# Chunked attention with a gated convolution on one core: the first head-pair group taken by halves, the start of a written-out order rearranged, and 27 GpSimd steps given a wait on VectorE

## The chip, the cores and the metric

The kernel runs on one core of a Trainium2 chip. The metric is the device time of one execution in microseconds (us); several runs of each kernel are made, and the median is compared. Four compute engines of the core appear below by the names of the profile: PE is TensorE (PEld its weight loads), DVE is VectorE, ACT is ScalarE, POOL is GpSimd. SP is the queue that issues every DMA of this kernel.

## What is computed

Attention inside chunks of 64 tokens, then a gate from a causal convolution of five taps and two projections:

```python
scores = scale * np.matmul(q_c, k_c.transpose(0, 1, 2, 4, 3))
scores = scores - np.max(scores, axis=-1, keepdims=True)
attn = np.exp(scores)
attn = attn / (np.sum(attn, axis=-1, keepdims=True) + 1e-09)
out = np.matmul(attn, v_c)
...
for k in range(K):
    gate_pre += conv_w[k][None, None, :] * xp[:, k:k + S, :]
gate = 1.0 / (1.0 + np.exp(-gate_pre))
val = x @ w_val
return (gate * val @ w_out).astype(np.float32)
```

q, k and v have 8 batches, 8 heads, 576 tokens and 64 features in float32; x is the attention's output with the heads side by side (512 features). The weights are 512 x 512 and arrive as 64-bit floats that the kernel turns into 32-bit ones itself.

## The kernel before

The 4608 tokens are taken in nine groups `g` of 512 tokens (0 to 8), and the 512 features in two pairs of 128-row blocks, `p` = 0 and 1. One (g, p) is called a pair here. The program is a list of short pieces, `ORDER`, 1034 of them, run in the order in which they are written. A piece is a name and numbers, and each engine executes its own instructions in that order. Nothing is reordered afterwards, so the table alone sets who stands behind whom on each engine. `SLOTS` gives every tile its buffer, also by hand: `z` tiles are 128 x 1024 in SBUF, `b` tiles are PSUM banks. A piece that reuses a buffer waits for the last reader of what was there. All instructions go through one helper, `run` (line 139 of the profile), so every row of the profile carries that line, and the tiles tell the rows apart.

The pieces of one pair, in the order of its data:

- `lq`, `lk`, `lv`: DMAs of q, k and v, 512 KB each (256 KB for a half). SP lets eight DMAs be under way; a ninth waits until the first has landed.
- `S g p b`: scores of one half b (16 products of 64 x 64, which the trace records as 32 matmuls).
- `mx`: the row maximum (DVE). Then one of two ways to the exponentials: `sb` subtracts the maximum (DVE) and `ex` takes one exponential over all (ACT); or `ng` negates the maximum (DVE) and `ea` takes eight or sixteen exponentials of 64 columns with the maximum as bias and the row sums as a by-product (ACT).
- `sm` (sum and reciprocal on DVE) or `rc` / `ra` and `rr` after `ea`: one over the row sums.
- `nm`: exponentials times that (POOL). `T`: transposes of the result (PE). `ec`: copy out of PSUM (ACT).
- `A`: attention times v (PE). `xr`, `xd`: the result as a rounded high part (ACT) and the rest (DVE); `xc`: a plain copy for the convolution (ACT, or DVE as `xcD`).
- `V g m c`: three (or, with a fourth number, one) products of 128 x 128 by 512 for the value projection; `P` the same for the output projection; `vc`, `gs`, `gr`, `gd`, `oc`, `st`: the gate, its two parts, the output copies and stores.
- `k0`, `k`, `kk`: the five taps (ACT for the first, DVE for the others), `sg` the sigmoid.

The weights go through `lw` (load), `w1` to `w4` (bits of the 64-bit float to a 32-bit one; `w2` on ACT, the others on DVE), `w5` and `w8` (the remainder), `w6` (rounded high part), `wa` and `wb` or `Q` and `wc` (the low part, the second way by PE). A letter `D` behind a name means that the piece runs on DVE. `n c` behind it is the matrix (`v` or `o`) and its quarter.

In the kernel before, pair (0, 1) goes by halves from the scores to the values, with `ng`/`ea` for both halves, and pair (0, 0) goes as a whole: one `mx`, one `sb`, one `ex`, one `sm`, one `nm`, one `T`, one `A`. `W 9 22` and `W 3` are products of a constant tile that no result needs.

The tables before and now both end in the same 602 pieces; what differs lies ahead of these.

Of the kernel before, what the change touches and what calls it, by code (L numbers as in the profile page):

```python
# [18 lines left out]
ORDER = """zw,lw v 1,zr 1,zr 0,lc,zi,zs 0,zs 1,lw v 3,lw v 2,w1 v 1,w5 c 0,w1 c 0,w2 v 1,w3 v 1,w5 v 1,w4 v 1,w2 c 0,w3 c 0,w5 v 3,  # L19
w7 v 1,w1 v 3,w6 v 1,w8D v 1,w2 v 3,w4 c 0,w3 v 3,W 9 22,Q v 1,lk 0 1 0,lq 0 1 0,w1 v 2,w4 v 3,w2 v 2,w3 v 2,w5 v 2,w6D v 3,  # L20
S 0 1 0,lk 0 0 0,lk 0 1 1,lq 0 1 1,lq 0 0 0,lk 0 0 1,lq 0 0 1,w4 v 2,wc v 1,mx 0 1 0,w6 v 2,w7 c 0,ng 0 1 0,w7 v 2,ea 0 1 0,ra 0 1 0,
W 3,S 0 1 1,w8D v 2,S 0 0 0,mx 0 1 1,w8D c 0,w9,ng 0 1 1,w7 v 3,S 0 0 1,lw v 0,lk 1 0,lq 1 0,lv 0 1,lw o 3,ea 0 1 1,ra 0 1 1,
rr 0 1 0,Q v 2,w8 v 3,mx 0 0,nm 0 1 0,sb 0 0,Q v 3,w5 v 0,w1 v 0,ex 0 0,T 0 1 0,w3 v 0,rr 0 1 1,S 1 0 0,wc v 2,sm 0 0,
nm 0 1 1,S 1 0 1,ec 0 1 0,w2 v 0,A 0 1 0,lk 1 1,lq 1 1,lv 0 0,lv 1 0,wc v 3,mx 1 0,T 0 1 1,nm 0 0,xr 0 1 0,ec 0 1 1,
V 0 2 2 0,sb 1 0,V 0 3 2 1,w5 o 3,A 0 1 1,xc 0 1 0,xr 0 1 1,w4 v 0,T 0 0,xc 0 1 1,xd 0 1 0,V 0 2 3 0,w6D v 0,V 0 3 3 0,
ec 0 0,V 0 2 3 1,w1 o 3,S 1 1 0,w7 v 0,ex 1 0,xd 0 1 1,A 0 0,w8 v 0,k0 0 2,sm 1 0,S 1 1 1,wa v 0,xc 0 0,V 0 0 2 0,V 0 2 2 1,
V 0 0 3 1,V 0 0 2 1,xr 0 0,mx 1 1,V 0 1 2 0,nm 1 0,V 0 0 3 2,V 0 3 3 1,k0 0 0,V 0 3 2 2,V 0 2 3 2,xd 0 0,V 0 3 1 0,
V 0 1 2 1,V 0 0 0 0,V 0 3 3 2,V 0 3 0 0,lw o 0,lw o 2,lw o 1,w5 o 0,k0 0 3,ng 1 1,k 0 0 1,T 1 0,k0 0 1,wbD v 0,V 0 0 0 2,
w2 o 3,V 0 3 2 0,k 0 0 2,V 0 2 1 1,ec 1 0,V 0 2 0 0,V 0 0 1 0,k 0 3 1,V 0 1 0 0,V 0 2 0 1,ea 1 1,V 0 2 0 2,w3 o 3,V 0 2 1 2,
k 0 1 1,V 0 3 1 1,V 0 0 2 2,V 0 1 1 1,w4 o 3,V 0 3 0 1,V 0 2 2 2,V 0 3 1 2,w1 o 1,A 1 0,k 0 0 3,w7 o 3,w1 o 0,V 0 1 3 2,  # L30
# [7 lines left out]
xd 2 0,vc 1 1,S 3 1 0,w4 o 0,S 3 1 1,ec 2 1,waD o 3,V 2 0 0,gs 0 0,xc 2 0,A 2 1,w6 o 0,w7 o 0,V 2 2 0,gs 0 1,xr 2 1,V 2 0 1,
lk 8 1,lq 5 1,w8 o 0,xd 2 1,V 2 1 0,V 2 2 1,ex 3 0,xcD 2 1,wa o 0,V 2 3 2,k0 1 0,V 2 3 0,sm 3 0,wb o 0,gr 0 0,S 4 0 0,
S 4 0 1,k0 1 2,mx 3 1,nm 3 0,V 2 2 2,gr 0 1,V 2 0 2,mx 4 0,k0 1 1,V 2 0 3,w6 o 2,hc 0 0,ng 3 1,hc 1 0,sb 4 0,hc 0 1,V 2 2 3,  # L40
wb o 3,ea 3 1,V 2 1 3,gdD 0 0,V 2 1 2,T 3 0,k 1 1 1,V 2 1 1,lv 4 0,lk 5 1,lk 7 0,lq 4 1,lk 4 1,lv 3 0,lk 5 0,lv 8 0,waD o 2,
V 2 3 1,wbD o 2,V 2 3 3,gdD 0 1,ec 3 0,S 4 1 0,S 4 1 1,rc 3 1,vc 2 0,k 1 1 2,A 3 0,ex 4 0,nm 3 1,mx 4 1,P 0 2 0,w5 o 1,
# [624 lines left out]
```

## Time and profile before

| | before |
|---|---|
| runs | 279.8, 280.34, 280.35 us; median 280.34 |
| span of the profiled execution (its first to its last instruction) | 279.6 us |
| its own time | not measured apart; the three runs lie 0.2 to 0.75 us above the span |
| PE busy | 268.9 us, 96% |
| DVE, ACT, POOL busy | 239.5, 198.7, 59.4 us |
| chain that ended last | PE 89%, DMA 8% |
| DMA | 42.46 MB, about 406 GB/s up to 49 us |
| granted PE clock | 1.00 over the span |

The page gives, for one profiled execution, the busy time of each engine, the span in slices, the DMA queues, and the chain of waits followed back from the last instruction. A matmul's end in the trace is modelled, so its duration (some 400 ns for 512 columns) is longer than the distance from one start to the next (some 230 ns): what PE can do is read from starts. "Issue" is idle time for which the profile shows no releaser.

### The profile page before, as it was taken

How to read it: one execution, taken by the hardware profiler on the slowest of the kernel's cores; microseconds unless marked ns; L12 is line 12 of the kernel's file. 1: busy time of each engine (PE TensorE's matmuls, PEld its weight loads, DVE VectorE, ACT ScalarE, POOL GpSimd, SP SyncE). 2: the span in 40 equal slices, each digit the busy share in tenths (PEclk: the TensorE clock that was granted, in tenths of full speed). 3: DMA queues.
4: the chain of work that ended last, by engine and by line, in shares of the span. 5: the costliest groups of instructions: out<-in, count | busy, mean ns of one | idle time of the engine just before them, and what ended most of it. 6: DMA issues, size and time to landing. Idle time of an engine off the chain costs nothing.

```text
span 279.6 us, 7851 instructions
## 1 busy us (share of the span) xinstructions
PE 268.9 (96%) x3370; PEld 216.6 (77%) x3370; DVE 239.5 (86%) x303; ACT 198.7 (71%) x368; POOL 59.4 (21%) x58
## 2 busy tenths in 40 slices
PE   6598999999998999999999999999999999999995
PEld 3366778887886888888888888888888888888884
DVE  3979999999999988989898998999999998996020
ACT  5899999999997988895958588837644544614402
POOL 1056242049294003061335001100000000300000
PEclk9999999999999999999999999999999999999999
DMA  6999999763831649540082000000000000050656
GB/s 224 395 409 406 406 407 409 290 225 108 281 149 37 192 150 338 189 131 30 2 292 88 2 5 2 0 0 2 0 0 0 4 0 0 16 212 0 241 209 225
DMA packets 14754, 42.46 MB, mean 152 GB/s; under 512 B 1536, under 2 KB 1792, under 8 KB 14720
## 3 DMA queue, kind: packets, MB, share of 16 engines
q1 hardware_dynamic: 14720, 41.97, 40.7%
q8 instruction: 26, 0.43, 0.6%
q14 instruction: 8, 0.07, 0.1%
HBM read 32.53 MB, written 9.44 MB: 150 GB/s over the span
## 4 chain that ended last, share of the span: by engine, by line
PE 89%; DMA 8%; issue 1%; SPq 0%; ACT 0%
PE b L139 89%; DMA z<-in_v 4%; DMA z<-in_moe_w_val 2%; DMA z<-in_q 2%; SPq L139 0%; ACT z L139 0%
## 5 line engine op out<-in xcount | busy, mean ns | idle before, releaser
L139 PE MATMUL b<-z,v_hi 128*128 128x512 f32 x288 | 97.3, 403 | 1.3 <-issue 1.1
L139 PE MATMUL b<-o_hi,z 128*128 128x512 f32 (+1 forms) x296 | 94.5, 391 | 0.0
L139 DVE SCALAR_TENSOR_TENSOR ys<-ys,cw 128x511 f32<-128x511 f32 (+7 forms) x104 | 84.5, 863 | 0.1
L139 ACT COPY z<-b 128x1024 f32<-128x1024 f32 (+2 forms) x53 | 50.3, 970 | 38.3 <-PE b L139 35.5
L139 PEld LDWEIGHTS b<-z,v_hi 128*128 128x128 f32 x288 | 53.8, 188 | 14.5 <-issue 1.7
L139 PEld LDWEIGHTS b<-o_hi,z 128*128 128x128 f32 x296 | 55.1, 188 | 12.6
L139 PE MATMUL b<-o_lo,z 128*128 128x512 f32 (+1 forms) x148 | 57.4, 388 | 0.0
L139 PE MATMUL b<-z,v_lo 128*128 128x512 f32 x144 | 55.9, 394 | 0.0
L139 POOL TENSOR_TENSOR z<-e_row,rs 128x1024 f32<-128x1024 f32 (+1 forms) x15 | 27.0, 1804 | 47.2 <-DVE rs L139 17.0
L139 PEld LDWEIGHTS b<-o_lo,z 128*128 128x128 f32 x148 | 27.8, 188 | 5.9
L139 PEld LDWEIGHTS b<-z,v_lo 128*128 128x128 f32 x144 | 27.1, 188 | 5.4
L139 POOL TENSOR_TENSOR z<-ys,z 128x1024 fp32r<-128x1024 f32 x4 | 10.0, 2527 | 96.9 <-ACT z L139 96.9
L139 ACT ACTIVATE ys<-ys 128x1024 f32<-128x1024 f32 x16 | 16.8, 1059 | 11.0 <-DVE ys L139 10.8
L139 ACT ACTIVATE e_row<-b,mx 128x64 f32<-128x64 f32 x80 | 23.7, 345 | 0.4 <-DVE mx L139 0.4
L139 DVE TENSOR_TENSOR z<-b,z 128x1024 fp32r<-128x1024 f32 (+1 forms) x19 | 22.0, 1161 | 2.3 <-ACT z L139 1.3
L139 ACT CAST z<-ys 128x1024 fp32r<-128x1024 f32 x16 | 16.5, 1048 | 9.0 <-DVE ys L139 9.0
L139 DVE TENSOR_REDUCE mx<-b 128x16 f32<-128x1024 f32 (+1 forms) x19 | 21.6, 1144 | 1.3 <-PE b L139 1.1
L139 PEld LDWEIGHTS b<-z,z 64*64 64x64 f32 x960 | 15.7, 135 | 7.8 <-DMA z<-in_k 2.6
L139 PE MATMUL b<-z,z 64*64 64x64 f32 x960 | 17.6, 221 | 3.7 <-DMA z<-in_q 3.0
L139 ACT CAST z<-b 128x1024 fp32r<-128x1024 f32 (+1 forms) x19 | 18.7, 991 | 2.1 <-PE b L139 2.1
L139 ACT ACTIVATE ys<-ys,cw 128x512 f32<-128x512 f32 (+1 forms) x25 | 19.2, 811 | 0.0
L139 ACT ACTIVATION_READ_ACCUMULATOR e_row<-b,mx 128x1 f32 x80 | 19.0, 238 | 0.0
(74 smaller groups left out, 308.3 us busy)
## 6 DMA issues: line engine op xcount, KB each, us to landing
out<-z SPq DMA_DIRECT2D x16, 512.0 KB, 3.7
z<-in_q SPq DMA_DIRECT2D x10, 512.0 KB, 7.2
z<-in_v SPq DMA_DIRECT2D x9, 512.0 KB, 5.0
ys<-in_v SPq DMA_DIRECT2D x9, 512.0 KB, 10.1
ys<-in_k SPq DMA_DIRECT2D x9, 512.0 KB, 7.3
z<-in_k SPq DMA_DIRECT2D x7, 512.0 KB, 9.4
ys<-in_q SPq DMA_DIRECT2D x6, 512.0 KB, 10.2
z<-in_moe_w_val SPq DMA_DIRECT2D x4, 512.0 KB, 5.4
```

Source lines behind the costliest of these rows:

```text
L139: return tc.keep_in_program_order(fn(*args, **kwargs))
```

## The change

- Pair (0, 0) goes by halves too: `mx`, `sb`, `ex`, `sm`, `nm`, `T`, `ec`, `A`, `xr`, `xd`, `xc` and its `lv` are two pieces each. Its `xc` runs once on DVE and once on ACT.
- Half 0 of pair (0, 1), and the pair (2, 0), go to the exponentials in a third way: `mh` splits the maximum into two rounded parts (two small DVE steps), `M` subtracts them from the scores in PSUM by four matmuls against minus the identity, and `exM` takes one exponential straight from PSUM. `M 0 1 0` has 256 columns each, `M 2 0` 512. This replaces `ng`, `ea`, `ra`, `rr` there, and `sb`, `ex` in (2, 0). Half 1 of (0, 1) keeps `ng` and `ea`, with `rc` for `ra` and `rr`.
- Weights: `w1G` is `w1` on POOL (value quarter 0, output quarters 0, 1, 2); `w58` is `w5` and `w8` in one DVE step (value quarter 1, output quarters 1, 2, 3); `w6`, `wa`, `wb` of some quarters change engine. One `nm` (3, 1) and one `k0` go to DVE, two `xc` (2, 1) and (3, 0) to ACT.
- The pieces ahead of the common tail stand in another order, SP's loads among them: q ahead of k, both ahead of value quarter 0; the halves of v (0, 0) ahead of k and q (1, 1); the loads of groups 2 and up mixed differently; v (1, 0) four loads later than before, counted in bytes.
- `SLOTS` is new throughout, and the tile `ys` holds the buffers from 28 up and no longer from 20 up.
- `BEHIND`: 27 pieces on POOL (`gd`, `nm`, `w1G`, `w8`, `wa`, `wb`) wait in addition until a named DVE piece has ended.

```diff
-ORDER = """zw,lw v 1,zr 1,zr 0,lc,zi,zs 0,zs 1,lw v 3,lw v 2,w1 v 1,w5 c 0,w1 c 0,w2 v 1,w3 v 1,w5 v 1,w4 v 1,w2 c 0,w3 c 0,w5 v 3,
...
+ORDER = """zw,lw v 1,zr 1,W 9 22,lc,w3 c 0,w5 c 0,w1 v 1,w2 v 1,w1 c 0,w2 c 0,w3 v 1,w4 v 1,w7 v 1,lw v 3,lw v 2,w1 v 3,w4 c 0,lq 0 1 0,
...
-ALONE = 20
+BEHIND = {
+    "nm 0 0 0": "sm 0 0 1", "nm 0 0 1": "sm 0 0 1", "w8 v 0": "w7 v 0", "wa v 0": "xd 0 1 1", "nm 1 0": "sm 1 0",
+    "w1G o 1": "xd 0 0 1", "nm 1 1": "rc 1 1", "w1G o 0": "xd 1 0", "w1G o 2": "w3 o 1", "nm 2 0": "w3 o 2",
+    "nm 2 1": "rc 2 1", "w8 o 0": "mx 3 0", "wa o 2": "w58 o 2", "nm 3 0": "sm 3 0", "wa o 1": "mx 4 1",
+    "wb o 1": "sb 4 1", "nm 4 0": "sm 4 0", "nm 4 1": "sm 4 1", "gd 1 1": "k 2 0 3", "gd 2 0": "nmD 5 1",
+    "gd 2 1": "mx 6 0", "nm 6 1": "sm 6 1", "nm 6 0": "sm 6 0", "nm 7 0": "sm 7 0", "nm 8 0": "sm 8 0",
+    "nm 7 1": "sm 7 1", "gd 3 1": "k 8 2 2",
+}
+
+ALONE = 28
...
+    def w58(n, c, b=None):
+        run(V.scalar_tensor_tensor, out=rest(n, c, b)[1], in0=part(raw[n, c][0], b), scalar=2.0**-52,
+            in1=part(wt[n, c], b), op0=ALU.mult, op1=ALU.mult)
...
-                            rhs=kk[r, b, c], start=True, stop=True, skip_group_check=True)
+                            rhs=kk[r, b, c], start=each or (first and u == a == 0), stop=True, skip_group_check=True)
...
+        if piece in BEHIND:
+            sync = mybir.DependencyInfo(mybir.DependencyClass.Sync, mybir.DependencyReason.DATA)
+            tc.add_manual_dep(made[begun].ins, ends[BEHIND[piece]].ins.name, sync, reason="behind")
```

`mh`, `less` (the piece `M`) and `exm` (`exM`) stood in the kernel before without being called.

PE, from the first transposes to the values of pair (0, 0), before. `b_308` and `b_419` hold the transposes of pairs (0, 1) and (0, 0), `b_356` and `b_399` the values of (0, 1), `b_459` those of (0, 0), `b_439` scores of (1, 1), `b_393` value projections.

```order
L139 MATMUL b_308<-ident,z_296 128x128 x4
L139 MATMUL b_393<-z_390,v_hi 128x512
L139 MATMUL b_393<-z_390,v_lo 128x512
L139 MATMUL b_399<-z_353,z_274 64x64 x16
L139 MATMUL b_419<-ident,z_388 128x128 x8
L139 MATMUL b_393<-z_390,v_hi 128x512 x2
L139 MATMUL b_393<-z_390,v_lo 128x512
L139 MATMUL b_439<-z_373,z_375 64x64 x16
L139 MATMUL b_459<-z_434,z_377 64x64 x32
L139 MATMUL b_439<-z_373,z_375 64x64 x16
```

The same place in the change. `b_304` and `b_404` hold the transposes of (0, 1) and (0, 0), `b_360` and `b_386` the values of (0, 1), `b_418` value projections.

```order
L147 MATMUL b_304<-ident,z_302 128x128 x4
L147 MATMUL b_310<-z_294,z_296 64x64 x32
L147 MATMUL b_304<-ident,z_302 128x128 x4
L147 MATMUL b_360<-z_350,z_358 64x64 x16
L147 MATMUL b_386<-z_350,z_358 64x64 x16
L147 MATMUL b_404<-ident,z_383 128x128 x8
L147 MATMUL b_418<-z_416,v_lo 128x512
L147 MATMUL b_418<-z_416,v_hi 128x512
```

Both pairs' transposes now stand ahead of the value projections. Five more projections follow the last row, then the two halves of the values of (0, 0): seven projections instead of five stand ahead of them, and the scores of (1, 1), which surrounded them, come behind.

DVE, from the first maximum on, in the change (`b_164`, `b_183` are the scores of the halves of (0, 1), `b_224`, `b_258` of (0, 0)):

```order
L147 TENSOR_REDUCE mx_204<-b_164 128x8
L147 CAST mr_206<-mx_204 128x8
L147 TENSOR_TENSOR mr_206<-mx_204,mr_206 128x8
L147 TENSOR_SCALAR z_159<-z_159 128x512
L147 TENSOR_REDUCE mx_215<-b_183 128x8
L147 TENSOR_TENSOR z_221<-z_221,z_159 128x512
L147 TENSOR_SCALAR mx_215<-mx_215 128x8
L147 TENSOR_REDUCE mx_248<-b_224 128x8
L147 TENSOR_REDUCE rs_254<-e_row_65 128x8
L147 RECIPROCAL rs_254<-rs_254 128x8
L147 TENSOR_TENSOR e_row_66<-b_224,mx_248 128x2x4x64
L147 TENSOR_REDUCE mx_275<-b_258 128x8
```

The maximum of (0, 0) is taken in two pieces of half the width, and the sum of half 0 of (0, 1), which ACT delivered before, stands between them.

POOL, first steps of the change with the waits (`z_302` is the normalised pair (0, 1), `z_383` the pair (0, 0), `z_356` the value quarter 0 on its way):

```order
L147 TENSOR_TENSOR z_252<-z_252,z_130 128x512 [waits DMAHW3_49,DVE_49,Activation_49]
L147 TENSOR_TENSOR z_302<-e_row_65,rs_254 128x2x256 [waits DVE_49,PE_49]
L147 TENSOR_TENSOR z_302<-e_row_65,rs_278 128x2x256 [waits DVE_49,Activation_49]
L147 TENSOR_SCALAR z_356<-z_352 128x512 [waits DMAHW3_49,DMAHW6_49,DMAHW0_49,PE_49]
L147 TENSOR_TENSOR z_383<-e_row_66,rs_291 128x2x256 [waits DVE_49,DMAHW4_49,PE_49,Activation_49]
L147 TENSOR_TENSOR z_383<-e_row_66,rs_377 128x2x256 [waits Activation_49]
```

The `TENSOR_SCALAR` (`w1G v 0`) is new on POOL and stands ahead of both halves of (0, 0), which were one step of 1024 columns before.

## Rows read from the trace of the kernel before

**Rows 1.** The page: span, and busy time of each engine.
```profile
span 279.6 us, 7851 instructions
PE 268.9 (96%) x3370; PEld 216.6 (77%) x3370; DVE 239.5 (86%) x303; ACT 198.7 (71%) x368; POOL 59.4 (21%) x58
```

**Rows 2.** Busy time by stretch: length, five engines, PE clock, DMA share, GB/s.
```profile
14.00:21.00 7.00, 6.32 (x144) 4.32 (x143) 5.51 (x10) 6.93 (x27) 3.73 (x4) 1.00 1.03 408
...
28.00:84.00 56.00, 55.83 (x1033) 45.70 (x1031) 53.31 (x76) 54.42 (x146) 25.43 (x20) 1.00 0.75 284
...
200.00:280.00 80.00, 76.67 (x342) 62.28 (x340) 56.14 (x60) 32.65 (x36) 2.91 (x1) 1.00 0.21 79
```

**Rows 3.** The chain of waits in order of time: start, length, what.
```profile
13.77 11.88 DMA z<-in_v
...
25.78 5.95 PE b L139 x118
```

**Rows 4.** PE's timeline, 24 to 32 us: start, length, what, idle before it.
```profile
24.66 0.69 PE L139 MATMUL b<-z,z 64*64 64x64 f32 x32
25.78 1.63 PE L139 MATMUL b<-z,z 64*64 64x64 f32 x96 [0.43 <-DMA z<-in_v]
27.34 0.50 PE L139 MATMUL b<-z,v_hi 128*128 128x512 f32 x1
...
31.90 0.50 PE L139 MATMUL b<-z,v_hi 128*128 128x512 f32 x1 [0.17 <-issue]
```

**Rows 5.** DVE's timeline, 10 to 21 us.
```profile
10.10 0.69 DVE L139 SCALAR_TENSOR_TENSOR z<-z 128x512 uint32<-128x512 uint32 x1
10.70 0.68 DVE L139 TENSOR_REDUCE mx<-b 128x8 f32<-128x512 f32 x1
...
17.70 0.20 DVE L139 RECIPROCAL rs<-rs 128x8 f32<-128x8 f32 x1
...
20.09 0.25 DVE L139 RECIPROCAL rs<-rs 128x16 f32<-128x16 f32 x1
```

**Rows 6.** POOL's timeline, 14 to 23 us.
```profile
14.17 1.27 POOL L139 TENSOR_TENSOR z<-z,z 128x512 fp32r<-128x512 f32 x1 [12.78 <-ACT e_row L139]
15.39 1.04 POOL L139 TENSOR_TENSOR z<-e_row,rs 128x512 f32<-128x512 f32 x1
...
20.58 1.90 POOL L139 TENSOR_TENSOR z<-e_row,rs 128x1024 f32<-128x1024 f32 x1 [1.55 <-PE b L139]
```

**Rows 7.** DVE's timeline, a one-input step on 512 columns.
```profile
8.48 0.43 DVE L139 TENSOR_SCALAR z<-z 128x512 f32<-128x512 f32 x1 [0.49 <-DMA z<-in_moe_w_val]
```

**Rows 8.** ACT's timeline, 19 to 20 us.
```profile
19.09 0.59 ACT L139 COPY z<-b 128x512 f32<-128x512 f32 x1
19.57 0.64 ACT L139 ACTIVATE z<-z 128x512 f32<-128x512 f32 x1
```

**Rows 9.** PE's timeline: matmuls of 512 and of 256 columns.
```profile
79.90 0.40 PE L139 MATMUL b<-o_lo,z 128*128 128x512 f32 x1
80.13 0.40 PE L139 MATMUL b<-o_hi,z 128*128 128x512 f32 x1
...
270.66 0.28 PE L139 MATMUL b<-o_lo,z 128*128 128x256 f32 x1
270.77 0.52 PE L139 MATMUL b<-o_hi,z 128*128 128x256 f32 x2
```

**Rows 10.** PE's timeline, 83 to 86 us.
```profile
82.03 1.16 PE L139 MATMUL b<-ys 64*64 64x64 f32 x64
83.01 1.11 PE L139 MATMUL b<-z,ys 64*64 64x64 f32 x64
...
85.68 0.50 PE L139 MATMUL b<-z,v_hi 128*128 128x512 f32 x1 [0.90 <-issue]
```

**Rows 11.** DVE's timeline: four taps at 87 us, and four at 242 us.
```profile
87.35 2.73 DVE L139 SCALAR_TENSOR_TENSOR ys<-ys,cw 128x511 f32<-128x511 f32 x4
...
242.29 4.90 DVE L139 SCALAR_TENSOR_TENSOR z<-tails,cw,z 128x512 f32<-128x512 f32 x4
```

**Rows 12.** POOL's timeline, 200 to 280 us.
```profile
242.40 2.91 POOL L139 TENSOR_TENSOR z<-ys,z 128x1024 fp32r<-128x1024 f32 x1 [66.32 <-ACT z L139]
```

More of the change, by code (lines that the diff above doesn't have):

```diff
@@ L38 @@
[L38 to L42, printed above, removed]
@@ new lines @@
+V 2 0 0,hc 1 0,V 2 0 1,ex 3 0,wa o 0,wb o 0,xd 2 1,mx 4 0,lv 4 0,k0 1 0,xc 2 1,V 2 3 1,V 2 1 2,lk 4 1,sm 3 0,hc 0 0,V 2 2 0,
+gr 0 0,lv 4 1,sb 4 0,V 2 0 3,V 2 3 2,S 3 1 1,S 3 1 0,mx 3 1,ng 3 1,V 2 2 1,gdD 0 0,lv 3 1,V 2 1 0,nm 3 0,w58 o 3,T 3 0,wbD o 2,
+k0 2 2,w6 o 3,w7 o 1,V 2 3 3,gr 0 1,k 1 1 1,gdD 0 1,V 2 2 3,k 1 1 2,lv 3 0,ea 3 1,rc 3 1,nmD 3 1,w58 o 1,V 2 1 3,V 2 0 2,
+V 2 1 1,V 2 2 2,lk 7 0,ec 3 0,waD o 3,V 2 3 0,vc 2 1,vc 2 0,k0D 1 2,ex 4 0,S 4 1 1,wbD o 3,A 3 0,hc 2 1,lk 8 1,xc 3 0,S 4 1 0,
@@ L241, in wb @@
-    def wb(n, c, on=G):
-        run(on.tensor_tensor, out=kept_in(wl, n, c), in0=unit(wt[n, c], n), in1=unit(wr[n, c], n), op=ALU.add)
-    def wq_sum(n, c):
-        w_ps[n, c] = unit(bank()[:, 0], n)
-        for i, (lhsT, rhs) in enumerate(((ident, wq[n, c].bitcast(F32)), (signed[:, 1], kept_in(wh, n, c)),
-                                         (signed[:, 0], wr[n, c].bitcast(F32R)))):
-            run(E.matmul, w_ps[n, c], lhsT=lhsT, rhs=rhs if i == 1 else unit(rhs, n), start=i == 0, stop=i == 2)
@@ new lines, in wb, with wq_sum @@
+    def wb(n, c, b=None, on=G):
+        run(on.tensor_tensor, out=kept_in(wl, n, c, b), in0=unit(part(wt[n, c], b), n, b), in1=unit(part(wr[n, c], b), n, b), op=ALU.add)
+    def wq_sum(n, c, b=None):
+        if (n, c) not in w_ps:
+            w_ps[n, c] = bank()[:, 0]
+        ps = unit(part(w_ps[n, c], b), n, b)
+        run(E.matmul, ps, lhsT=ident, rhs=unit(part(wq[n, c], b).bitcast(F32), n, b), start=True, stop=False)
+        run(E.matmul, ps, lhsT=signed[:, 1], rhs=kept_in(wh, n, c, b), start=False, stop=False)
+        run(E.matmul, ps, lhsT=signed[:, 0], rhs=unit(part(wr[n, c], b).bitcast(F32R), n, b), start=False, stop=True)
@@ L254, in w9, with wc @@
+    def wc(n, c, b=None, copy=S.copy):
+        run(copy, out=kept_in(wl, n, c, b), in_=unit(part(w_ps[n, c], b), n, b))
     def w9():
@@ L262, in sc @@
         own = (g, p) in HALVES
-        if own or b == 0:
+        each, first = (g, p, b if own else None) not in LESS, own or (g, p) not in s_ps
+        if own or (g, p) not in s_ps:
             ps = bank().rearrange("p h (b c k) -> p h b c k", b=2, c=4)
@@ L439, in xc @@
         else:
-            if not b:
+            if (g, p) not in xs:
                 xs_at[g, p] = []
```

250 lines of the change are left out of this document (140 added, 110 removed), and 12 rows, old and new, of the table z.

## The prediction

> **What bounds the kernel now.** First the busy line of the page: PE is busy for 268.9 of 279.6 us, so at most some 11 us can be won without taking matmuls away [rows 1]. Then the stretches, to see where these 11 us lie. From 28 to 84 us PE has 0.17 us idle, and DVE and ACT are nearly full beside it (53.3 and 54.4 of 56 us); at the end there are 3.3 us, which hold the last copies and stores and which the change does not touch; the rest lies ahead of 28 us [rows 2]. So the kernel is a head of about 28 us, in which PE waits for its first inputs, and a long row of matmuls at PE's own pace. Whatever the head saves comes off the total, and every matmul that is added behind it is paid in full. Last the chain: it leaves PE for the last time at 25.64 us, where PE waits for v of pair (0, 0); from then on it is PE alone [rows 3]. The time 28 us is also where I compare: at 27.34 us PE has done all scores of (1, 1), the values of (0, 0) and five value projections, and goes on with projections [rows 4].
>
> The three runs lie 0.2 to 0.75 us above the profiled span of 279.6; I sum against the span and carry the difference over to the median, 280.34. About 0.2% (0.56 us) is what a measurement of this kernel tells from no change.
>
> **The head, step by step.** Durations are those of the rows; steps on DVE start 0.60 us apart for 512 columns though each lasts 0.68 [rows 5].
> - Start of the first maximum: 10.70 us before. Now a 20-column piece that waits for the convolution weights stands first on DVE; I put it at 10.9. The first remainder takes one DVE step of 0.69 either way.
> - DVE from there to the reciprocal of half 1 of (0, 1): eight steps of 512 columns (4.8), one of 0.35, the two small `mh` steps that wait for each other (0.4), two other small ones (0.2), two reciprocals of 0.25: 6.25 us, so 17.2. In the kernel before it ended at 17.9 [rows 5].
> - The two sums of (0, 0), 0.85 each: done at 18.9, where the one sum of the whole pair ended at 20.34 [rows 5].
> - POOL: the second half of (0, 1), 1.04, up to 18.4 with the hand-over. Then `w1G v 0`, for which this trace has no row. Its bounds are DVE's one-input step of 0.43 [rows 7] and POOL's two-input step of 1.27; I take 1.04, that of a POOL step of the same width with one full operand [rows 6]. Then the halves of (0, 0), 1.04 each: 20.5 and 21.5. Before, the whole pair ran from 20.58 to 22.48 [rows 6].
> - ACT multiplies behind `w1G` (0.64), then copies the transposes of half 1 (0.59) [rows 8]: 20.6. PE does the second half of the values of (0, 1), the transposes of (0, 0) by 22.2, seven projections at 0.23 [rows 9], and the values of (0, 0) in two times 0.52 (96 matmuls took 1.56) [rows 4]: 25.2 us with two hand-overs of 0.14 (landing 25.64, start 25.78) [rows 3].
> - v of (0, 0) has two loads of 512 KB fewer ahead of it, 2.6 us at 406 GB/s [rows 2]. It lands near 23 us and is hidden by the projections; if it came as before, at 25.6, about 1.5 us would be lost.
>
> By 25.2 us PE has two projections more than before at 27.34 (0.46) and lacks the scores of (1, 1) (1.05). The same work is thus done at 25.8: the head is shorter by 1.5 us, 1.0 at the dear end of the unknown prices and 1.9 at the cheap end. I take 1.4.
>
> The Trainium skill (GPSIMD Engine Reference, Engine selection) holds that two-input steps cost about twice VectorE's time on GpSimd and one-input ones about the same. POOL's 1.27 against DVE's 0.68 agrees with the first half; of the second no row exists. By it `w1G` would be near 0.43, and the estimate of the sum 0.4 us lower.
>
> **What is added and moved behind the head.**
> - `M 0 1 0` (four matmuls of 256 columns, 0.12 each) runs inside the head and is in the count above. `M 2 0` is four of 512 columns at 0.23 [rows 9]: +0.93 us of PE, hidden by nothing.
> - DVE from 28 to 84 us: three `w58` (+1.8), `nmD` (+1.1), `wbD`, `w6D`, `k0D`, one `xcD` (+2.2), less `sb 2 0`, two `xcD`, `waD` and three `w1` (-5.0). That is level, beside 2.7 us of slack [rows 2]. ACT loses three `w5`, two `w6` and one `k0` and gets two copies: about 1.5 us less. Both stay hidden under PE, but barely. If DVE grew by over 2.7 us, PE would wait for the rest of it.
> - The 27 waits: most name a step that POOL waits for anyway (its sum or its remainder). The others, as `wa v 0` behind `xd 0 1 1`, hold POOL by under 1 us, and POOL is busy for 25 of these 56 us [rows 2]. Behind `wa v 0` only the normalising of (1, 0) queues, whose transposes PE asks for some 2 us later. I cost the waits at nothing; the bound is 0.5 us.
> - New buffers and load order: hidden by prefetch, but for the rival below.
> - Two idle spots of PE have no releaser: 0.17 at 31.90 and 0.90 at 85.68, the second behind 128 short matmuls in a row [rows 4, 10]. Both places have as many short matmuls now. I leave both as they are, with bounds of -1.1 and +1.0.
>
> Sum: -1.4 + 0.93 = -0.47 us: span 279.1, median **279.9 us**. Its own range is 279.3 to 280.5.
>
> **Rivals.**
> 1. *The idle spots go.* The blank 1.07 us falls away because the short matmuls come in other company (scores of (5, 1) are now split around the values of (3, 1)), or `w1G` is cheap. For it: no data are late there. Against it: the same number of short matmuls in the same 6 us. 280.34 - 0.47 - 1.07 = 278.8.
> 2. *VectorE is held by GpSimd (slower).* Where POOL's 2.91 us step began beside four taps, the taps took 4.90 us, against 2.73 for four at 87 us: 2.2 us lost [rows 11, 12]. Three of the new `w1G` steps and the moved `w8`/`wa` run among the taps of groups 0 and 1, between 28 and 50 us. If they hold DVE for their length, 3 x 1.04 and some of the `wa`, DVE's slack of 2.7 us is gone and PE waits for the remainder, 1 to 2 us: 281.2. It decides from 2.7 us of DVE time on. The Trainium skill (SBUF — State Buffer, the rule on the shared port pair) says the same as a lock: a DVE step with two SBUF inputs and a GpSimd step exclude each other for the whole instruction. The taps' 4.90 agrees. Against the rival: the added waits start POOL behind a DVE step that is followed by one reading PSUM.
> 3. *A load is late.* v of (1, 0) has 2 MB more ahead of it than before: near 32 us at 406 GB/s, and PE asks for it near 32.5. Half a microsecond of margin: 280.9 if the queue is 1 us late.
> 4. *The halves do nothing.* PE takes both transposes of (0, 0) back to back, so that only the second half counts, and the small steps eat what is won: head shorter by 0.9 or less, 280.4.
>
> **How the numbers follow.** Forecast 0.44 (0.14 of it below 279.78, 0.29 within 0.2%, 0.01 above); rival 1 0.27, all faster; rival 2 0.16, slower; rival 3 0.08 (0.06 slower, 0.02 the same); rival 4 0.05, the same. Faster 0.41, same 0.36, slower 0.23. The range leaves out the far half of rivals 1 and 2: 278.7 to 281.2.
>
> **What would show it.** Right: POOL's two half steps of (0, 0) end near 20.5 and 21.5 us; the values of (0, 0) run near 24 to 25.2 us with no idle time put down to a load; PE has 3378 matmuls, eight more; PE's last matmul ends 0.5 us earlier. Wrong: PE idle for DVE or ACT between 28 and 84 us (rival 2), for a load of v near 32 us (rival 3), or blank spots that add up to something far from 1.1 us (rival 1 or its opposite).

## The result, and the profile after

The change made the kernel slower: median **284.44 us** of 4 runs (283.89 to 284.84), against 280.35 of 4 runs of the kernel before (279.8 to 280.7) beside it. The ratio is 1.014 with a 95% interval of 1.0114 to 1.0166. The forecast was 279.9 us, and its range ended at 281.2. Below, each ratio is to runs of the kernel before that were made beside it, with medians of 280.66 to 281.03 us. The ratios leave out runs in a slower state of the chip (four of the twelve of e12_after_long, two of the six of e1_four), while the medians take them in.

The top of the page after: PE is busy 3.1 us longer than in [rows 1], and the span is 3.5 us longer. Not all of the busy time is added work: the warming products at the start alone took 5.20 us, 4.16 before.

```profile
span 283.1 us, 7871 instructions
PE 272.0 (96%) x3378; PEld 219.1 (77%) x3378; DVE 242.3 (86%) x321; ACT 195.5 (69%) x352; POOL 55.1 (19%) x59
...
q8 instruction: 26, 0.43, 0.6%
```

The busy times by stretch after, which answer to [rows 2]; columns as there.

```profile
28.00:35.00 7.00, 5.74 (x88) 4.55 (x87) 5.27 (x10) 5.52 (x13) 2.65 (x3) 1.00 1.02 404
35.00:84.00 49.00, 49.00 (x883) 40.10 (x881) 46.65 (x70) 47.51 (x133) 15.76 (x15) 1.00 0.66 248
84.00:90.00 6.00, 4.82 (x139) 4.09 (x139) 5.88 (x7) 5.65 (x7) 5.08 (x4) 1.00 0.40 135
```

From 35 to 84 us PE has no idle time at all, though DVE and ACT are loaded as before. The new idle time lies in two short places, 28 to 35 and 84 to 90 us. What ended PE's waits from 20 us on (total, times, longest):

```profile
PE b L147 <- issue: 3.2, 3, 1.3
PE b L147 <- ACT z L147: 1.6, 2, 0.9
```

The three waits put down to "issue" have no releaser in the profile. In the kernel before there were two, 1.07 us together [rows 4, 10]. PE's timeline has the three at 25.9, 31.5 and 86.0 us; one falls inside the values of (0, 0), one into transposes, one into scores of (5, 1). The first row is of the transposes of (0, 0):

```profile
22.99 1.09 PE L147 MATMUL b<-ident,z 128*128 128x128 f32 x8
...
25.65 0.46 PE L147 MATMUL b<-z,z 64*64 64x64 f32 x16
26.82 0.93 PE L147 MATMUL b<-z,z 64*64 64x64 f32 x48 [0.71 <-issue]
...
33.02 0.38 PE L147 MATMUL b<-ident,z 128*128 128x128 f32 x2 [1.26 <-issue]
...
87.40 0.33 PE L147 MATMUL b<-ys 64*64 64x64 f32 x4 [1.19 <-issue]
```

To add this up I use a measure of lost time: the start of a matmul, less the time that all matmuls ahead of it need at the pace at which they follow one another without a wait (0.232 us for 512 columns, 0.118 for 256, 0.110 for a transpose, 0.0147 for a 64x64, 0.134 for a change between kinds). By it the three blanks after are 0.91, 1.42 and 1.39 us, and the two before 0.33 and 1.06. The last matmul starts at 276.39 before and 279.71 after, 3.32 us later:

| part of the 3.32 us | us |
|---|---|
| work of PE: `M 2 0` 0.93, `M 0 1 0` 0.47, changes between kinds 0.13 | +1.53 |
| lost up to 28.4 us: 12.23 before, 12.43 after (0.91 of it the first blank) | +0.20 |
| lost behind 28.4 us: the other two blanks 2.81, against 1.39 before | +1.42 |
| lost behind 28.4 us: the rest | +0.17 |

One number of the sum's base was read wrongly: the profiled execution of before is hardly one of the three that were listed. (The 3.3 us at the end are too many as well: the last stretch of [rows 2] reaches 0.4 us beyond the span. Nothing rests on it.) In after and the runs below the time lies 1.7 to 2.0 us above the span, so a span of 279.6 most likely belongs to a run of some 281.4 us. That is the difference between 3.5 us by the traces and 4.1 by the medians.

### The profile page after: what moved, and what is told of

Same layout as the page of the kernel before. It is cut to its first block, busy times and chain, and to the rows that moved or that the text cites. A ratio compares the mean times of both kernels' runs of the same rounds, so it can differ in the third digit from the quotient of the medians.

```text
span 283.1 us, 7871 instructions
## 1 busy us (share of the span) xinstructions
PE 272.0 (96%) x3378; PEld 219.1 (77%) x3378; DVE 242.3 (86%) x321; ACT 195.5 (69%) x352; POOL 55.1 (19%) x59
## 4 chain that ended last, share of the span: by engine, by line
PE 90%; DMA 5%; issue 1%; SPq 1%; ACT 1%; POOL 0%; POOLq 0%
PE b L147 90%; DMA z<-in_v 3%; DMA z<-in_q 3%; SPq L147 1%; ACT z L147 1%; POOL z L147 0%; POOLq L147 0%
## 5 line engine op out<-in xcount | busy, mean ns | idle before, releaser
L147 ACT COPY z<-b 128x1024 f32<-128x1024 f32 (+2 forms) x66 | 61.1, 946 | 39.9 <-PE b L147 37.6
L147 DVE SCALAR_TENSOR_TENSOR z<-z,cw,z 128x511 f32<-128x511 f32 (+3 forms) x80 | 55.6, 741 | 0.0
L147 POOL TENSOR_TENSOR z<-z,z 128x1024 fp32r<-128x1024 f32 (+2 forms) x7 | 13.7, 1970 | 113.7 <-PE b L147 67.9
L147 ACT ACTIVATE z<-z 128x1024 f32<-128x1024 f32 (+3 forms) x24 | 20.2, 863 | 17.7 <-DVE z L147 17.6
L147 DVE SCALAR_TENSOR_TENSOR ys<-ys,cw 128x1022 f32<-128x1022 f32 (+7 forms) x32 | 31.1, 1006 | 0.0
L147 PEld LDWEIGHTS b<-z,z 64*64 64x64 f32 x1344 | 21.9, 135 | 9.0 <-ACT z L147 3.8
L147 PE MATMUL b<-z,z 64*64 64x64 f32 x1344 | 24.7, 220 | 3.8 <-ACT z L147 1.6
L147 DVE TENSOR_TENSOR z<-z,z 128x1024 f32<-128x1024 f32 (+2 forms) x21 | 24.6, 1193 | 3.3 <-ACT z L147 1.9
L147 ACT ACTIVATE e_row<-b,mx 128x64 f32<-128x64 f32 x72 | 21.4, 350 | 0.6 <-DVE mx L147 0.5
L147 PE MATMUL b<-ident,z 128*128 128x128 f32 x144 | 19.1, 275 | 1.3 <-issue 1.3
```

Of the source, the lines that this page charges most:

```text
L147: made.append(tc.keep_in_program_order(fn(*args, **kwargs)))
```

## The experiments

Four theories stood, of which several can hold at once:

- **A, instruction supply.** A blank is PE waiting for its own instructions. The trace's eighth DMA queue carries 26 packets of 16 KB for PE's 6817 instructions (weight loads and matmuls and the rest), and the blanks lie at PE's instructions number 704, 960 and 3008, which are all 448 plus a multiple of 256 (counted over PE's records in the trace, from the first).
- **B, data.** A blank is a wait for data whose releaser the profile doesn't show. Then it belongs to a piece of work, not to a number.
- **C, the 27 waits**, or DVE held by GpSimd.
- **D, the head's order.** Two orders cost what the halves should have won: the copy `ec 0 1 0` stands behind `T 0 1 1`, and `w5`, `w1G`, `w2` of value quarter 0, whose load is late, stand ahead of copies.

### A against B: other instruction numbers (e7_shift)

```diff
-W 9 22
+W 9 38
-W 3
+W 3 16
```

`W` is a run of products that keep PE busy and whose result nobody uses. The edit puts 64 instructions of PE more (32 weight loads and matmuls) among the first work.

> The changed kernel with 32 more of the short warming matmuls (64 columns, 0.03 us each) ahead of the first scores, 64 PE instructions more, in stretches where PE is idle (up to 0.3 us of them may show). Theory A: the blanks stay at instructions 704, 960 and 3008 of PE's stream and so move 32 matmuls forward in the work: the first from the values of (0, 0) into the row of value projections ahead of them (24 us), the second ahead of the transposes of (1, 0) (29 to 30 us, and longer there, 2 us or more), while the third goes or shrinks, since its packet is now asked for before the three loads of 80 us are issued. Sum between -0.5 and +1.0 us: 284 to 285.4. Theory B: the blanks stay at the same tiles (values of (0, 0), transposes of (1, 0), taps' scores at 86 us), 284.4 to 284.7.

Measured: 285.09 us (5 runs), 1.015 [1.0128, 1.0172]; profiled span 282.8. PE's timeline at the numbers 704, 960, 3008 and 4032:

```profile
24.42 1.03 PE L140 MATMUL b<-ident,z 128*128 128x128 f32 x8 [1.21 <-issue]
...
31.72 0.57 PE L140 MATMUL b<-z,z 64*64 64x64 f32 x22 [1.29 <-issue]
...
86.24 0.65 PE L140 MATMUL b<-ys 64*64 64x64 f32 x32
...
125.72 0.60 PE L140 MATMUL b<-ident,z 128*128 128x128 f32 x4 [0.49 <-issue]
```

The blanks stayed at the numbers and went to other work: from the values of (0, 0) to the transposes ahead of them, from transposes to 64x64 products. The place of the third blank, the scores at 86 us, runs through, and a new one stands at 125 us, where no other kernel of the study has one. B would have kept them at their work. B falls.

The same reading for all 14 traces. For each number the last byte of its instruction packet was set against PE's own records there: the start of the record with that number, and the start of the next one. Nine of the rows:

```
kernel           number  packet's end  PE there  next instruction  behind the packet
before              960      30.42       31.45        31.90              1.48
before             3008      84.10       84.39        85.67              1.57
after               704      25.51       25.89        26.82              1.31
after               960      31.48       31.48        33.02              1.53
after              3008      86.00       85.99        87.39              1.40
e7_shift            704      22.81       23.14        24.42              1.62
e7_shift            960      30.15       30.21        31.72              1.57
e7_shift           4032     124.45      124.95       125.72              1.27
e13_best           1472      45.33       44.35        46.70              1.37
```

There are 24 such stops of over 0.4 us in the 14 traces. In each of them the next instruction comes 1.27 to 1.62 us behind the packet's last byte, whatever the work is. In the other 327 crossings PE comes to the number at least 0.97 us behind the packet and goes on without a stop of over 0.4 us. Nor are there blanks elsewhere: behind 5 us the 14 timelines of PE have 24 waits without a releaser, and all 24 are these stops. So A: a packet has to be in some 1.0 to 1.6 us ahead, and PE stops for what is missing of that. The Trainium skill (Runtime: NRT & Kernel Launch, Instruction fetch mechanics) describes this supply: blocks of 16 KiB, 256 instructions each, which an engine's sequencer fetches through a DMA queue of its own while the block before runs. The 26 packets agree. It adds that a crossing is "mostly hidden"; here three of them cost 3.7 us.

### What makes a packet late: loads held back (e3_hold)

```diff
-T 4 0,lv 8 0,k 1 2 1
+T 4 0,k 1 2 1
...
-lq 8 0,lk 6 0,lk 6 1,st 0 1
+lk 6 1,lv 8 0,lq 8 0,lk 6 0,st 0 1
```

`lk 6 1` waits for its buffer, and the other three now wait behind it on SP's queue.

> The changed kernel with the loads of v (8, 0), q (8, 0) and k (6, 0) put behind that of k (6, 1), so that they are issued at about 88 us instead of 79.9 to 80.8. Theory A: nothing is under way at 80 to 85 us, the packet of the instruction queue that began at 85.1 us begins near 81, and the blank stretch of 1.4 us at 86 us goes: 283.0 us. Theories B and C: the blank stays; 284.4.

Measured: **282.59 us** (6 runs), 1.0061 [1.0045, 1.0077]; profiled span 280.7. The DMA view of 78 to 84 us, after (packets, MB, share of the 16 engines) and then this kernel:

```profile
q1 hardware_dynamic: 297, 1.10, 51.3%
q8 instruction: 1, 0.02, 1.4%
```

```profile
q8 instruction: 1, 0.02, 0.9%
```

And PE's timeline of the same scores as at 87.40 us after:

```profile
84.79 0.65 PE L140 MATMUL b<-ys 64*64 64x64 f32 x32
```

With the loads gone the packet for number 3008 begins 0.28 us before PE comes to 2752; after, it began 2.24 us behind it. The blank is gone, and the median is 1.85 us lower, more than the 1.39 us of that blank. In this profile the stop at 704 is absent too, which the edit doesn't touch (packet's end 24.41, reached at 26.66), and the one at 960 has become shorter (0.79 against 1.53). So the early stops also differ from execution to execution.

### Fewer loads under way (e1_four)

```diff
+        if name in ("lq", "lk", "lv", "lw", "lc"):
+            loads.append(made[-1])
+            if len(loads) >= 14:
+                tc.add_manual_dep(loads[-1].ins, loads[-1 - 4].ins.name, ...)
```

> Theory A (instruction supply): the three blank stretches of PE in the changed kernel (0.93 at 26.8 us, 1.53 at 33.0, 1.40 at 87.4) stand at instructions 704, 960 and 3008 of PE's stream, each right behind the end of a 16 KB packet of the instruction queue (25.5, 31.5 and 86.0 us), whose transfer had begun 5 to 7 us after PE came to its instruction 144 of the same 256. The packets stand behind the loads under way. With four loads under way instead of eight, from the 14th load on, A expects the packets to start 3 to 4 us earlier in 15 to 50 us, the first two blanks to go (-2.3 us) and the third to stay, since only three loads are under way there: 282.0 to 282.5 us. Theory B (the blanks are waits for data whose releaser the profile does not show): they stay where they are; 284.4, or slower if loads land later. Theory C (the 27 waits, or DVE held by GpSimd): no change, 284.4.

Measured: 289.26 us (285.84 to 290.92, 6 runs), 1.0254 [1.0209, 1.0299]. Two stretches of the profiled execution, a run of 285.84:

```profile
14.00:21.00 7.00, 5.53 (x112) 3.56 (x110) 6.14 (x13) 5.07 (x23) 4.36 (x5) 1.00 0.87 296
...
35.00:42.00 7.00, 5.91 (x138) 4.73 (x131) 4.84 (x8) 5.10 (x20) 2.50 (x2) 1.00 1.01 400
```

A miss. Four loads move 296 GB/s from 14 to 21 us, where 409 were moved after, so data come later. And the stops did not go: those at 704 and 960 did, and 1216, 1472 and 3008 stop for 1.31, 0.94 and 1.68 us. The packet of 1216 began 6.9 us behind number 960, though only four loads were under way. So the number of loads under way does not decide it. Nor was the traffic less where that packet came late: from 35 to 42 us the four loads moved 400 GB/s. What decides the moment while loads run stays open.

### C: without the 27 waits (e4_noties)

```diff
-BEHIND = {
-    "nm 0 0 0": "sm 0 0 1", "nm 0 0 1": "sm 0 0 1", "w8 v 0": "w7 v 0", ...
-}
+BEHIND = {}
```

> The changed kernel without the 27 added waits. Theory A: within 0.4 us of 284.4, with the three blanks at the same instructions of PE. Theory C (the waits hold POOL and what is queued behind it): faster by 1 us or more. A third reading, that the waits keep DVE free of GpSimd as meant: slower by 1 to 2 us, and the taps of groups 0 and 1 longer than 0.75 us each.

Measured: 284.38 us (6 runs), 1.0132 [1.0096, 1.0168], against 1.014 with them. C falls, within the 1 us or so that the intervals leave: the waits cost nothing that can be measured, and save nothing. The taps of 508 to 511 columns between 36 and 80 us take 0.74 us each with the waits and without. The stops at 960 and 3008 stand there too; the second is this one:

```profile
85.83 0.33 PE L133 MATMUL b<-ys 64*64 64x64 f32 x4 [1.19 <-issue]
```

### The burst of short matmuls in the kernel before (e9_before_burst)

```diff
-S 5 1 0,...,A 3 1,...,P 0 3 3,...,P 0 2 1,...,P 0 3 1
+P 0 3 3,P 0 2 1,P 0 3 1,S 5 1 0,...,A 3 1
```

This is the kernel before, with three output projections moved ahead of 128 short matmuls (scores of (5, 1), values of (3, 1)).

> The kernel before with one edit: three pieces of the output projection of group 0 (nine matmuls of 512 columns) stand ahead of the scores of (5, 1) and the values of (3, 1), the 128 short matmuls in a row, and no longer behind them. Theory A: PE then takes 2.1 us longer from its instruction 2704 to 3008, the packet that ended at 84.1 us ends ahead of that, and the blank of 1.06 us at 85.68 us goes, with the same work: 279.8 us (ratio 0.9965 or less). Theory B (the blank is a wait for data of the projection that follows): the blank stays or moves with it, 280.9.

Measured: 281.96 us (7 runs), 1.0047 [1.0027, 1.0068]. A miss: the blank shrank, from 1.06 to 0.75 in lost time, but did not go, and behind it PE waits for DVE:

```profile
86.21 0.34 PE L129 MATMUL b<-z,ys 64*64 64x64 f32 x7 [0.55 <-issue]
...
89.91 0.50 PE L129 MATMUL b<-z,v_hi 128*128 128x512 f32 x1 [0.61 <-DVE z L129]
```

The stop moved on in the work with the number, which speaks for A once more. PE took 3.62 us from number 2752 to 3008, against 2.35 before, so that 1.3 of the 2.1 us of moved work lie between the two numbers; and the packet began later too, 1.69 us behind PE's coming to 2752 against 1.19. Why the median is 1.3 us above that of the kernel before is explained by the wait for DVE only in part.

### D: the head in another order (e6_hold_head)

The kernel of e3_hold, and besides:

```diff
-wc v 2,S 1 0 0,S 1 0 1,nm 0 1 1,T 0 1 1,ex 0 0 1,wc v 3,ec 0 1 0,lw v 0,w5 v 0,w1G v 0,lv 0 1,A 0 1 0,sm 0 0 1,w2 v 0,
+wc v 2,S 1 0 0,S 1 0 1,ex 0 0 1,wc v 3,ec 0 1 0,nm 0 1 1,T 0 1 1,lw v 0,lv 0 1,A 0 1 0,sm 0 0 1,
...
-ec 0 0 0,V 0 3 2 0,...,ec 0 0 1,xd 0 1 0,xd 0 1 1,
+ec 0 0 0,ec 0 0 1,xd 0 1 0,xd 0 1 1,w5 v 0,w1G v 0,w2 v 0,V 0 3 2 0,...
```

> The changed kernel with the three loads held back, and with the head put right: the copy of the first half's transposes of (0, 1) stands ahead of the second half's transposes, and the three steps of value quarter 0 (w5, w1G, w2) stand behind the copies of (0, 0) and the remainders of (0, 1), so that neither POOL's halves of (0, 0) nor ACT's copies queue behind a load that lands at 19.3 us. Theory D (the head lost 1.4 us to these two orders): POOL's halves of (0, 0) end near 20.8 us and no longer at 22.15, the second values of (0, 1) near 21.6 and no longer at 23.0, the values of (0, 0) 1.0 to 1.5 us earlier; the time 281.2 to 281.6 us (ratio 1.001 to 1.003). Theory A adds: what PE wins here it can lose again at its instruction 704 or 960, whose packets come at their own time (23.3 to 25.5 and 30 to 31.5 us), so that the values end earlier and the time stays near 282.3. Rival (the head is bound by the loads of v, 20.6 us for (0, 1)): no step moves, 282.6.

Measured: **281.82 us** (10 runs), 1.0049 [1.0025, 1.0072], against 1.0061 for e3_hold; profiled span 279.4, 1.3 us shorter than that of e3_hold. GpSimd's, ACT's (the copy `ec 0 1 0`) and PE's timelines:

```profile
18.74 2.04 POOL L140 TENSOR_TENSOR z<-e_row,rs 128x512 f32<-128x512 f32 x2 [0.64 <-PE b L140]
20.75 0.67 POOL L140 TENSOR_SCALAR z<-z 128x512 f32<-128x512 f32 x1
```

```profile
17.72 0.66 ACT L140 COPY z<-b 128x512 f32<-128x512 f32 x1
```

```profile
20.94 1.09 PE L140 MATMUL b<-ident,z 128*128 128x128 f32 x8
...
30.20 1.09 PE L140 MATMUL b<-ident,z 128*128 128x128 f32 x8 [0.99 <-POOL z L140]
```

The copy begins 2.4 us earlier than in the change (20.15), GpSimd's half steps of (0, 0) 1.4 us earlier, and the transposes of (0, 0) 2.1 us earlier. By 24 us 9.66 us are lost, against 11.21 before and 11.19 after: the head gives 1.5 us in this order. D holds for the order; that the load is late has no part in it, as e12_after_long shows below. Of the 1.5 us 0.99 goes again at 30.20: the normalising of (1, 0) stands behind `wa v 0` on GpSimd, as in the change, begins at 28.24 (28.08 there), and is now too late for a PE that is earlier.

### The subtraction through PSUM undone (e5_hold_sub, e10_hold_sub_head)

```diff
-mh 2 0
+sb 2 0
-M 2 0,exM 2 0
+ex 2 0
```

In e5_hold_sub this is done to e3_hold, in e10_hold_sub_head to e6_hold_head.

> The changed kernel with the three loads held back as before, and with the pair (2, 0) as in the kernel before: the maximum subtracted by DVE (sb 2 0, ex 2 0) and not by the four matmuls M 2 0. If these matmuls are paid in full (four at 0.23 us), it is 0.9 us below the kernel with the loads alone held back, some 281.7 us (ratio 1.003 to the kernel before). If they are hidden, or if DVE's longer step makes PE wait, it is equal to it or slower: 282.6 us or more.

> The changed kernel with all three: loads held back, pair (2, 0) as before, head put right. If the terms add: 282.6 less 0.9 less 1.0 to 1.4, that is 280.3 to 280.7 us, level with the kernel before. If PE loses at its instruction 704 or 960 what the head wins: 281.5.

Measured: 283.05 us (6 runs), 1.0089 [1.0068, 1.0109], and 282.28 us (6 runs), 1.0061 [1.0037, 1.0084]. Misses, both: 0.93 us of matmuls fewer, and not faster. PE now waits there for ACT and DVE (e5_hold_sub):

```profile
44.22 2.33 PE L140 MATMUL b<-z,z 64*64 64x64 f32 x128 [0.44 <-ACT z L140]
...
49.05 0.73 PE L140 MATMUL b<-z,v_hi 128*128 128x512 f32 x2 [0.43 <-DVE z L140]
```

In lost time the two places cost 0.83 and 0.84 us, where e3_hold loses none. So `M 2 0` pays for itself: without it DVE has `sb 2 0` to do, and the delay comes through to PE.

### Other instruction numbers by fewer warming products (e12_after_long, e11_before_long and its repeat)

```diff
-W 9 22
+W 12
```

38 instructions of PE fewer, in the change (e12) and in the kernel before (e11, and e14 once more).

> The changed kernel with the same one number changed, nothing else. Theory A: the blanks of 1.5 us (instruction 960) and 1.4 us (3008) go, since both instructions now stand among long matmuls behind their present place, and that at 704 shrinks from 0.9 to 0.5 us or goes: 281 to 281.8 us (ratio 1.001 to 1.005). Theories B and C: 284.4 (1.014).

> The kernel before with one number changed: the warming products at the start are twelve of 512 columns and no longer nine of 512 and 22 of 64, about the same time (3 x 0.21 for 22 x 0.03 us) in 38 PE instructions fewer. Every instruction of PE behind them has a number lower by 38. Theory A: instruction 960 falls behind the transposes of (1, 0), into long matmuls, and 3008 four microseconds behind the 128 short matmuls; both blanks (0.33 at 31.9 us, 1.06 at 85.7) go, with the same work in the same order: ratio 0.995 to 0.997, some 279.4 us. Theory B (the blanks are waits of these matmuls): no change, 280.7.

> The kernel before with the twelve long warming products, once more, since its first interval (0.9959 to 1.0006) just reached 1. Theory A: again 0.2 to 0.4% below the kernel before, ratio 0.996 to 0.998. If the first run's 0.18% was chance: 0.999 to 1.001.

Measured: e12 **282.51 us** (281.15 to 285.76, 12 runs), 1.0052 [1.0024, 1.008]; e11 280.36 us (12 runs), 0.9982 [0.9959, 1.0006]; e14 280.49 us (12 runs), 0.9987 [0.997, 1.0005].

The change with 19 warming products less (38 instructions), and nothing else altered, is 1.9 us faster by the medians, not quite the 2.6 to 3.4 that were expected. The span on its page, its waits of PE from 20 us on, and PE at the three places of the blanks:

```profile
span 279.4 us, 7833 instructions
```

```profile
PE b L140 <- ACT z L140: 1.6, 2, 0.9
```

```profile
25.61 1.16 PE L140 MATMUL b<-z,z 64*64 64x64 f32 x64
...
30.00 1.09 PE L140 MATMUL b<-ident,z 128*128 128x128 f32 x8
...
83.40 0.65 PE L140 MATMUL b<-ys 64*64 64x64 f32 x32
```

No blank is left: 960 and 3008 now stand behind runs of long matmuls, and PE reaches both 3.5 us behind their packets. The span is 3.7 us shorter than after, which is what the three blanks cost there. The head has not changed: the transposes of (0, 0) start at 22.95, against 22.99. This profile is of the fastest of the 12 runs, and four of the 12 took 285.4 to 285.8 us, more than any run of the change. The others have no profile; that stops come back in them is likely, and not shown.

In the kernel before, the same edit takes both blanks away (no wait of PE from 28 us on in e11), and yet the time is hardly shorter, another miss: the head is later. The transposes of (0, 0) start at 24.01 in e11 and at 22.90 before, and the longest wait ahead of them is 2.2 us for a step on ACT that took 0.3 us of PE's time before:

```profile
PE b L129 <- ACT v_hi L129: 2.2, 1, 2.2
...
24.01 1.06 PE L129 MATMUL b<-ident,z 128*128 128x128 f32 x8 [0.33 <-DVE e_row L129]
```

e14's profiled span is 278.4, with 1.1 us at that wait and one stop of 0.46 at number 704. Both intervals take in 1, so this version is not shown to beat the kernel before.

### All together (e13_best)

e6_hold_head, with `wa v 0` behind `nm 1 0` and `W 12`.

> The changed kernel with the loads held back, the head put right, the normalising of (1, 0) ahead of the low part of value quarter 0 on POOL, and the same number changed. If the terms add: 281.8 (with the loads and the head) less 1.2 (PE's wait for the normalising of (1, 0) at 30 us) less 0.3 (the rest of the blank at 704): 280.3 us, ratio 0.998 to 1.000. If instruction supply then binds at 960 again: 281.5.

Measured: 283.52 us (6 runs), 1.0105 [1.0072, 1.0139]. A miss: the numbers now fall into other short matmuls, and PE stops three times (at 704, 1216 and 1472), once for over 2 us; this is in a run of 284.78, the second longest of the six. PE's timeline at the last two, and two stretches behind them:

```profile
38.55 0.34 PE L140 MATMUL b<-z,z 64*64 64x64 f32 x7 [0.56 <-issue]
...
46.70 0.69 PE L140 MATMUL b<-z,z 64*64 64x64 f32 x30 [2.13 <-issue]
```

```profile
48.00:50.00 2.00, 2.00 (x7) 1.52 (x6) 2.00 (x4) 0.60 (x2) 1.44 (x1) 0.50 1.02 406
...
52.00:54.00 2.00, 2.00 (x11) 1.58 (x10) 2.00 (x4) 2.00 (x16) 0.00 (x0) 1.00 0.89 358
```

Behind the long stop the granted clock is 0.50 for some 3.4 us, which costs PE another 1.6 us (eight products of 512 columns at 0.43 instead of 0.23). Improvements of the head don't add up with a shift of the numbers here: each edit moves the numbers to other work and other times. No version of the study is shown to be faster than the kernel before.

## Why the prediction was wrong, point by point

| step of the prediction | forecast | after |
|---|---|---|
| first maximum starts | 10.9 | 10.78 |
| reciprocal of half 1 of (0, 1) ends | 17.2 | 17.54 |
| sums of (0, 0) done | 18.9 | 19.14 |
| second half of (0, 1) on POOL ends | 18.4 | 18.73 |
| `w1G v 0` | 1.04 long, from 18.4 | 0.64 long, from 19.51 |
| halves of (0, 0) on POOL end | 20.5, 21.5 | 22.15 (the second) |
| copy of half 1 of (0, 1) on ACT done | 20.6 | about 22.3 |
| values of (0, 0) done | 25.2 | 27.6 (0.9 of it a blank) |
| lost time at 28 us, against before | -1.87 | +0.20 (-0.71 without the blank) |
| PE work added | +1.40 | +1.53 |
| blanks | as before, -1.1 to +1.0 | +2.3 |

**The sum's order of steps was right up to 19 us, within 0.35 us.** The rows after, DVE first, then POOL and ACT:

```profile
10.78 0.69 DVE L147 TENSOR_REDUCE mx<-b 128x8 f32<-128x512 f32 x1
...
17.34 0.20 DVE L147 RECIPROCAL rs<-rs 128x8 f32<-128x8 f32 x1
...
18.94 0.20 DVE L147 RECIPROCAL rs<-rs 128x8 f32<-128x8 f32 x1
```

```profile
17.69 1.04 POOL L147 TENSOR_TENSOR z<-e_row,rs 128x512 f32<-128x512 f32 x1 [1.31 <-DVE rs L147]
...
19.51 0.64 POOL L147 TENSOR_SCALAR z<-z 128x512 f32<-128x512 f32 x1 [0.77 <-PE b L147]
20.11 2.04 POOL L147 TENSOR_TENSOR z<-e_row,rs 128x512 f32<-128x512 f32 x2
```

```profile
20.15 0.58 ACT L147 COPY z<-b 128x512 f32<-128x512 f32 x1 [1.77 <-POOL z L147]
20.63 1.21 ACT L147 ACTIVATE z<-z 128x512 f32<-128x512 uint32 x2
21.72 1.08 ACT L147 COPY z<-b 128x512 f32<-128x512 f32 x2
```

**"ACT multiplies behind `w1G` (0.64), then copies the transposes of half 1 (0.59): 20.6" failed first; the copy was done at about 22.3.** The chain left out two things of the new order. ACT's copy of half 0 stands behind the transposes of half 1, which share its PSUM bank, and PE takes these at 19.40, behind 64 score products; so half 0, transposed by 18.0, was not taken until 20.15:

```profile
17.94 1.53 PE L147 MATMUL b<-z,z 64*64 64x64 f32 x64
19.40 0.66 PE L147 MATMUL b<-ident,z 128*128 128x128 f32 x4
```

Then two multiplications of value quarter 0 (`w5`, `w2`; 1.21 us) stand ahead of the copy of half 1, where the prediction counted one of 0.64. PE waits 1.6 us for the two copies, and the transposes of (0, 0) stand behind these waits. The head falls 1.2 us short of the 1.87 even without its blank, and this order is the cause: e6_hold_head, which changes it, loses 1.5 us less than the change by 24 us. It moves the copy and the three steps of value quarter 0 together; what each gives alone was not tried.

**"New buffers and load order: hidden by prefetch" was wrong for POOL, and cost PE nothing.** Value quarter 0 landed at 19.3 us, where it had landed at 15.0 before, and `w1G v 0` waited 0.77 us, with both halves of (0, 0) behind it. In e12_after_long it landed at 18.05, and `w1G` follows the step ahead of it without a wait:

```profile
18.99 0.66 POOL L140 TENSOR_SCALAR z<-z 128x512 f32<-128x512 f32 x1
```

Yet PE's waits for ACT are the same 1.6 us there, and the transposes of (0, 0) start at the same time.

**"I leave both as they are" failed by more.** The bound of +1.0 was too small: the blanks grew by 2.3 us, the sign of being wrong that the prediction itself gave. The prediction's ground, that both places hold as many short matmuls as before, was the wrong thing to count. What decides is where in the work PE's instruction numbers 448 + 256 n fall, and how late the packet of that number comes, later beside loads. The 38 instructions of e12_after_long and the four moved loads of e3_hold show both. Rival 1 had the blanks going away; its place was right and its sign was not.

**`w1G` was mis-sized, and in the cheap direction.** 0.64 us, and 0.65 to 0.67 for the later ones, lie between the two ends (0.43 and 1.27). The Trainium skill (GPSIMD Engine Reference, Engine selection) calls one-input steps on GpSimd "roughly line-rate", which the prediction took for VectorE's time. It is not: here GpSimd takes 1.5 times VectorE's 0.43 [rows 7].

**Right:** `M 2 0` as 0.93 us of PE that nothing hides. That taking it out would give this back was never claimed, and e5_hold_sub shows that it doesn't. Right too: eight matmuls more, the 27 waits at nothing (e4_noties), and DVE and ACT hidden from 35 to 84 us, so that rival 2 did not come about. Five taps take 3.38 us there, 0.68 each, at a time when POOL does nothing, so that its price was not put to the test:

```profile
50.40 3.38 DVE L147 SCALAR_TENSOR_TENSOR z<-z,cw,z 128x508 f32<-128x508 f32 x5
```

Rival 3 did not occur: v of (1, 0) landed at 32.3 us as worked out, and no wait is put down to it. Rival 4 did in part: PE takes both transposes of (0, 0) in one row of eight at 22.99.

**The forecast's mechanism, halves that shorten the head, was thus right, and its price about right, for an order that the change does not have.** In the order of e6_hold_head it gives 1.5 us of the 1.87, against 1.53 us of added matmuls: even then, and without any blank, no change that could be measured.

## What to carry to other kernels

A wait of PE without a releaser beside a burst of short matmuls can be its instruction supply: count PE's instructions to the place, and look whether it lies at a fixed step of 256 and what the loads did just before. Then hold back loads around the burst, or shift the count by some warming products, and measure with many runs, because any edit ahead of it shifts all later crossings. And before a half is counted as won, go through each engine's order for what stands ahead of its steps: two multiplications and one copy behind the other half's transposes took back 1.2 us of 1.87 here, while a load that was visibly late cost nothing.

## What the runs showed of the hardware

- **Packets of instructions come later beside loads.** With three loads taken away, the packet of number 3008 began 0.28 us ahead of PE's coming to the number before, and no longer 2.24 us behind it (e3_hold). Behind 120 us, where PE runs mostly long matmuls beside fewer loads, packets begin from 4.7 us ahead of PE's coming to the number before up to 1.2 us behind it (before and after). While loads move over 400 GB/s, up to 45 us, they begin 3.2 to 5.9 us behind it in these two, though a packet itself takes only 1.0 to 1.2 us there; over all 14 traces it is 0.4 to 6.9 us. 128 short matmuls are 256 instructions and take about 2 us, less than most of these delays.
- **A packet shows in the DMA view.** Between two of them, 25.6 to 30.4 us after, only loads run; the packet of number 960 comes at 30.4 (packets, MB, share):

```profile
q1 hardware_dynamic: 542, 1.97, 102.5%
```

```profile
q8 instruction: 1, 0.02, 5.9%
```

- **A stop can be followed by a lower clock.** In e13_best the granted clock was 1.00 up to 47.9 us, 0.50 up to 51.3 and 1.00 again behind that, so 1.2 GHz and then 2.4; products of 512 columns started 0.43 us apart in between, 0.23 behind. PE's longest idle time from 20 us on (2.13 us) stood ahead of it. The shorter stops after (up to 1.4 us) show a clock of 1.00 on both sides. That the stop brought the lower clock on is not shown by this one case.
